# Three steps of lag for the second product, an in-place subtraction in PSUM, two hand-written orders and a store on two queues

## The chip, the cores and the metric

The kernel runs on one NeuronCore of one Trainium2 chip. The metric is the device time of one execution in microseconds (us). Of the core's engines, TensorE (PE) multiplies into PSUM, VectorE (DVE) and ScalarE (ACT) do elementwise work on SBUF and PSUM, GpSimd (POOL) does elementwise work on SBUF, and SyncE (SP) issues the DMA transfers.

## The reference

Local attention with block summaries, then two feed-forward layers, all in fp32 (B 2, H 8, S 768, D 64, so 1536 tokens of width 512):

```python
scores_l = where(|i - j| < 16, q @ k.T / 8, -1e9)
scores_s = q @ max_over_32(k).T / 8 + log(32)
a = softmax(concat(scores_l, scores_s))
x = a @ concat(v, mean_over_32(v))          # 1536 x 512
h = x @ w_in                                # 512 -> 2048
x = (h - tanh(h)) @ w_out                   # 2048 -> 512
out = ((x @ w1) * (x @ w2)) @ w3 @ w_out2   # 512 -> 1024 -> 1024 -> 512
```

## The kernel before

Every large product is made of three float32r products of 512 columns, high x high, high x low and low x high (`split_mm`, lines 224 to 226). So each operand is first split in a high part (a cast, on ACT or POOL) and a low part (a subtraction, on POOL). Weights arrive as 64-bit words; each unit of 128 x 512 is put together by ACT and DVE (`start`, `dve`: two or three DVE operations), then split (`high`, `low`).

**Attention** goes through 24 groups g, three for each pair of heads, in about 27 steps. For one group: PE makes the scores (S), DVE the maxima (M0 to M3), ACT the exponentials (E0 to E3), DVE the reciprocal sum (R), POOL the scaled probabilities (PP, tile pr), PE their transposes (T, tile t), ACT a copy (PB, tile pt), PE the product with the values (V, tile av), ACT the high part of x (XH) and DVE the low part (XL). The tiles t and av have one buffer each, so V of a group waits until XL of the one before has read av. VB on PE and VC on ACT make the block means of v, K0 to K2 those of k, which POOL copies into the tile kt. Between these, PE folds w3 @ w_out2 in 32 parts (W0, W1) of six products (tile w34a); `PLAN["N34"]` tells how many parts a step takes. What each engine does in which order within a step is written out in `PLAN["L"]`, a list of tokens for steps 0 and 1, for 2 to 16 and for the rest.

**The middle** has 48 steps n, four or six slices f of w_in and w_out by three blocks of 512 tokens. `hidden(n)` makes h for one slice on PE, into one of three PSUM banks (tile ph), 12 products; `curve` makes h - tanh(h): ACT takes u = h*h, tanh, a polynomial's term sq and a mask mk, DVE takes h*u (line 714), h - tanh(h) (line 715), the polynomial (line 716) and, one step later, `copy_predicated` (line 698), which puts h - tanh(h) over the polynomial where the mask says so. Its result g is split into gh (ACT) and gl (POOL). `back(n - LAG)` multiplies with w_out, 12 more products (tile x2, x in the trace). LAG is 2 in the kernel before: PE runs hidden(n), then back(n - 2).

**The last stage** (m = 0 to 7) multiplies with w1, w2 and the folded w3 @ w_out2 by seven products in place of eight; `final` adds up the output banks o and stores them, the last one in two halves, a copy by ACT and one by DVE into one tile, both sent by SP. Engines work in program order; nothing reorders the instructions at run time.

Of the kernel before, what the change touches and what calls it, by code (L numbers as in the profile page):

```python
# [43 lines left out]
LAG = 2  # L44
# [7 lines left out]
PLAN = {"cuts": [2, 17], "N34": [0, 0, 0, 0, 0, 1, 2, 1, 1, 0, 2, 1, 2, 2, 2, 0, 0, 3, 3, 1, 1, 2, 1, 3, 1, 2, 3],  # L52
        "MORE": (15, 18, 22, 23), "MOREU": (20, 24, 26),
        "SIGN": (1, 3, 5, 7, 9, 11, 13, 15, 17, 19, 20, 21, 22, 23, 24, 25, 26, 27, 28, 29, 31, 32, 35, 37, 38, 39, 41, 43, 45, 47, 49, 51, 53, 55, 57, 59, 61, 63, 65, 67, 69, 71, 73, 75, 77, 79), "ACT": (0, 4, 8, 16, 22, 25, 27, 29, 33)}
PLAN["L"] = [
# [12 lines left out]
]  # L68
NEG = -8.0 * 1000000000.0
LOG_BLK = 8.0 * 3.4657359027997265  # L70

UMAX = 0.03125
SS, SB, GAM = 0.23012508654699032, 0.2896718893925817, 0.2494235093653836
# [981 lines left out]
```

## Time and profile before

| | us |
|---|---|
| three runs | 578.0, 579.14, 580.85 |
| median | 579.14 |
| profiled execution | 579.49 |
| its span, first to last instruction | 577.8 |
| what lies outside the span | 1.7 |
| PE busy in the span | 559.2 (97%) |

The profile is a record of every instruction of one execution, with the time for which each engine sat idle and what released it. A share of the span tells which engine is used most; where time can be had is told by its idle time, stretch by stretch. The granted clock is TensorE's, as a share of 2.4 GHz: 0.50 is the lower of its two levels, 1.2 GHz.

### The profile page before, as it was taken

How to read it: one execution, taken by the hardware profiler on the slowest of the kernel's cores; microseconds unless marked ns; L12 is line 12 of the kernel's file. 1: busy time of each engine (PE TensorE's matmuls, PEld its weight loads, DVE VectorE, ACT ScalarE, POOL GpSimd, SP SyncE). 2: the span in 40 equal slices, each digit the busy share in tenths (PEclk: the TensorE clock that was granted, in tenths of full speed). 3: DMA queues.
4: the chain of work that ended last, by engine and by line, in shares of the span. 5: the costliest groups of instructions: out<-in, count | busy, mean ns of one | idle time of the engine just before them, and what ended most of it. 6: DMA issues, size and time to landing. Idle time of an engine off the chain costs nothing.

```text
span 577.8 us, 9217 instructions
## 1 busy us (share of the span) xinstructions
PE 559.2 (97%) x3224; PEld 451.2 (78%) x3224; DVE 459.8 (80%) x881; ACT 336.4 (58%) x736; POOL 295.3 (51%) x259
## 2 busy tenths in 40 slices
PE   6898999999999999999999999999999999999997
PEld 5676777777788888888888888888887887888885
DVE  4887789987999999679999969999568587768610
ACT  4888798956978875567867566855233422213110
POOL 4776677753556556216555423457736554616220
PEclk9798999999999999999999999999999999999999
DMA  8987876441333232012323102223000100000021
GB/s 336 354 301 248 299 242 212 127 175 38 109 111 109 77 107 74 0 40 76 105 75 108 36 2 73 74 73 110 1 1 1 73 1 2 0 2 0 1 91 54
DMA packets 18526, 56.56 MB, mean 98 GB/s; under 512 B 1968, under 2 KB 4656, under 8 KB 18480
## 3 DMA queue, kind: packets, MB, share of 16 engines
q1 hardware_dynamic: 18480, 55.98, 29.1%
q8 instruction: 25, 0.41, 0.3%
q14 instruction: 21, 0.17, 0.1%
HBM read 51.64 MB, written 3.15 MB: 95 GB/s over the span
## 4 chain that ended last, share of the span: by engine, by line
PE 84%; DVE 6%; ACT 5%; POOL 2%; issue 2%; POOLq 0%; DVEq 0%; ACTq 0%
PE x L225 7%; PE x L224 7%; PE x L226 7%; PE ph L224 7%; PE ph L226 7%; PE ph L225 7%; PE p_w L224 5%; PE p_w L226 4%; PE p_w L225 4%; PE o L226 4%; PE o L224 4%; PE o L225 4%; PE w L226 2%; PE w L225 2%; PE w L224 2%
## 5 line engine op out<-in xcount | busy, mean ns | idle before, releaser
L229 POOL TENSOR_TENSOR gl<-g,gh 128x512 fp32r<-128x512 f32 x48 | 65.5, 1366 | 131.7 <-ACT gh L693 69.7
L186 POOL TENSOR_TENSOR wl<-dec,wh 128x512 fp32r<-128x512 f32 x72 | 111.5, 1550 | 13.8 <-ACT wh L179 12.4
L225 PE MATMUL x<-gl,wh 128*128 128x512 f32 x192 | 75.1, 391 | 2.2 <-POOL gl L229 2.2
L224 PE MATMUL x<-gh,wh 128*128 128x512 f32 x192 | 75.1, 391 | 1.0 <-ACT gh L693 0.9
L224 PE MATMUL ph<-xh,wh 128*128 128x512 f32 x192 | 74.9, 390 | 0.0
L226 PE MATMUL x<-gh,wl 128*128 128x512 f32 x192 | 74.8, 390 | 0.0
L225 PE MATMUL ph<-xl,wh 128*128 128x512 f32 x192 | 74.8, 389 | 0.0
L226 PE MATMUL ph<-xh,wl 128*128 128x512 f32 x192 | 74.8, 389 | 0.0
L148 DVE SCALAR_TENSOR_TENSOR dec<-raw,dec 128x512 uint32<-128x512 uint32 x48 | 62.8, 1308 | 1.5
L706 ACT ACTIVATE u<-ph 128x512 f32<-128x512 f32 x48 | 28.8, 599 | 47.2 <-PE ph L226 47.2
L714 DVE TENSOR_TENSOR g<-ph,u 128x512 f32<-128x512 f32 x48 | 32.8, 683 | 18.9 <-ACT th L707 18.7
L229 POOL TENSOR_TENSOR s_w<-s_w,s_w 128x512 fp32r<-128x512 f32 x16 | 22.9, 1446 | 43.5 <-ACT s_w L885 23.5
L179 ACT CAST wh<-dec 128x512 fp32r<-128x512 f32 x52 | 32.3, 622 | 21.3 <-DVE dec L148 21.2
L225 PEld LDWEIGHTS x<-gl,wh 128*128 128x128 f32 x192 | 36.1, 188 | 10.6 <-POOL gl L229 3.1
L698 DVE COPY_PREDICATED g<-mk,th 128x512 f32<-128x512 uint32 x48 | 40.9, 852 | 3.8
L224 PEld LDWEIGHTS x<-gh,wh 128*128 128x128 f32 x192 | 36.1, 188 | 9.6 <-ACT gh L693 1.8
L429 ACT ACTIVATE pr<-pr,nm 128x120 f32<-128x120 f32 x96 | 37.7, 396 | 7.5 <-DVE nm L424 7.5
L226 PEld LDWEIGHTS ph<-xh,wl 128*128 128x128 f32 x192 | 36.1, 188 | 7.5
L224 PEld LDWEIGHTS ph<-xh,wh 128*128 128x128 f32 x192 | 36.1, 188 | 7.5
L225 PEld LDWEIGHTS ph<-xl,wh 128*128 128x128 f32 x192 | 36.1, 188 | 7.4
L226 PEld LDWEIGHTS x<-gh,wl 128*128 128x128 f32 x192 | 36.1, 188 | 7.4
L716 DVE SCALAR_TENSOR_TENSOR g<-sq,g 128x512 f32<-128x512 f32 x48 | 39.0, 812 | 0.7 <-ACT sq L712 0.6
(163 smaller groups left out, 1424.9 us busy)
## 6 DMA issues: line engine op xcount, KB each, us to landing
raw<-w SPq DMA_DIRECT2D x32, 512.0 KB
raw<-w_in SPq DMA_DIRECT2D x16, 512.0 KB
raw<-w_out SPq DMA_DIRECT2D x16, 512.0 KB
vg<-vW SPq DMA_DIRECT2D x8, 768.0 KB
raw<-wo SPq DMA_DIRECT2D x8, 512.0 KB
kt<-kT SPq DMA_DIRECT2D x7, 544.0 KB
qt<-qT SPq DMA_DIRECT2D x7, 384.0 KB
out<-u_out SPq DMA_DIRECT2D x6, 256.0 KB
```

The costliest lines, as they stand in the source:

```text
L148: lambda tu=tu, su=su, lo=lo: stt(out=tu, in0=lo, scalar=29, in1=su, op0=ALU.logical_shift_right, op1=ALU.bitwise_or)])
L179: nc.scalar.copy(out=h, in_=self.t[n])
L186: nc.gpsimd.tensor_tensor(out=l, in0=self.t[self.n_low], in1=h[:, :].bitcast(F32), op=ALU.subtract)
L224: mm(out=acc, lhsT=lh, rhs=rh, start=start, stop=False)
L225: mm(out=acc, lhsT=lh, rhs=rl, start=False, stop=False)
L226: mm(out=acc, lhsT=ll, rhs=rh, start=False, stop=stop)
L229: eng.tensor_tensor(out=out, in0=x, in1=high.bitcast(F32), op=ALU.subtract)
L429: nc.scalar.activation(out=pr[g][:, i, :], in_=pr[g][:, i, :], func=AF.Exp, scale=-1.0, bias=nm[g][:, i:i + 1], accum_out=z[g][:, i, :1])
L698: nc.vector.copy_predicated(out=g, mask=mask[:, :].bitcast(U32), data=t)
L706: nc.scalar.activation(out=u, in_=ph, func=AF.Square)
L714: nc.vector.tensor_tensor(out=gn, in0=ph, in1=u, op=ALU.mult)
L716: nc.vector.scalar_tensor_tensor(out=gn, in0=sq, scalar=GAM, in1=gn, op0=ALU.add, op1=ALU.mult)
```

## The change

Five things. LAG becomes 3, with `NG2 = 3` buffers of gh and gl as before. DVE writes h - tanh(h) back into the bank ph, and `copy_predicated` reads it there, so that the bank stays in use until then. The orders `PLAN["L"]`, `N34` and the lists of which weight unit is taken by which engine are other ones; the middle's order is now a table too, `PLAN["MIDDLE"]`, with one row for each of the first eight steps and one for all others. In the last stage, for m of 3 and more, waiting weight units are split ahead of `w34_split`. The last output bank goes through two tiles; ACT issues the store of its half itself.

```diff
-LAG = 2
+LAG = 3
+NG2 = 3
-PLAN = {"cuts": [2, 17], "N34": [0, 0, 0, 0, 0, 1, 2, 1, 1, 0, 2, 1, 2, 2, 2, 0, 0, 3, 3, 1, 1, 2, 1, 3, 1, 2, 3],
+PLAN = {"cuts": [2, 17], "N34": [0, 0, 0, 0, 0, 2, 0, 2, 2, 0, 2, 1, 2, 1, 2, 0, 1, 2, 3, 1, 2, 1, 1, 3, 1, 2, 3],
...
+PLAN["MIDDLE"] = [
+    ["G", "U", "EV", "EV", "HID", "UT", "EV", "H", "EV", "SM", "MM", "RS", "BK", "C"],
...
+    ["HID", "ST", "H", "EV", "C", "U", "UT", "G", "SM", "MM", "L", "RS", "BK"],
...
-                nc.vector.tensor_tensor(out=t, in0=ph, in1=t, op=ALU.subtract)
...
+        def curve_m(n):
+            ph, u, sq, t, mask, gn = curves[n]
+            nc.vector.tensor_tensor(out=gn, in0=ph, in1=u, op=ALU.mult)
+            nc.vector.tensor_tensor(out=ph, in0=ph, in1=t, op=ALU.subtract)
+            nc.vector.scalar_tensor_tensor(out=gn, in0=sq, scalar=GAM, in1=gn, op0=ALU.add, op1=ALU.mult)
+
+        def curve_c(n):
+            ph, u, sq, t, mask, gn = curves[n]
+            nc.vector.copy_predicated(out=gn, mask=mask[:, :].bitcast(U32), data=ph)
...
+        for n in range(NS + LAG):
+            for tok in PLAN["MIDDLE"][min(n, len(PLAN["MIDDLE"]) - 1)]:
+                step(tok, n)
...
+                w = DM // 2
+                for i, tag, copy, q in ((0, "u", nc.scalar.copy, nc.scalar), (w, "gh", nc.vector.tensor_copy, nc.sync)):
+                    o = tmp(tag, f"out_{k}_{j}_{i}", NG2 if tag == "gh" else 2)
+                    copy(out=o[:, :w], in_=acc[k, j][:, i:i + w])
+                    q.dma_start(out=out[rows, i:i + w], in_=o[:, :w])
...
+            if m > 2:
+                wt.high()
+                wt.low()
             w34_split(m)
```

In the table's tokens HID is hidden(n), UT u and tanh, SM sq and mask, MM the three DVE operations, C `copy_predicated` of n - 1, G the split of n - 1, BK back(n - LAG), U, D, ST, H and L the weight units, EV and RS the accumulators.

The program of POOL at the start of attention (pr_1 is PP of group 1, kt_1 the block maxima of the second pair of heads, wl and wh the parts of a weight unit), before:

```order
L441 TENSOR_TENSOR pr_0_198<-pr_0_198,r_0_246 128x480
L365 COPY kt_1_166<-kb_1_278 128x12x24
L186 TENSOR_TENSOR wl_0_283<-dec_0_212,wh_0_282 128x512
L441 TENSOR_TENSOR pr_1_205<-pr_1_205,r_1_293 128x480
L177 CAST wh_1_309<-dec_1_262 128x512
L186 TENSOR_TENSOR wl_1_310<-dec_1_262,wh_1_309 128x512
```

and after:

```order
L455 TENSOR_TENSOR pr_0_189<-pr_0_189,r_0_248 128x480
L379 COPY kt_1_166<-kb_1_261 128x12x24
L455 TENSOR_TENSOR pr_1_207<-pr_1_207,r_1_291 128x480
L200 TENSOR_TENSOR wl_0_295<-dec_0_214,wh_0_294 128x512
L191 CAST wh_1_321<-dec_1_266 128x512
L200 TENSOR_TENSOR wl_1_322<-dec_1_266,wh_1_321 128x512
```

The scaled probabilities of group 1 have moved ahead of the low part of weight unit 0.

The program of PE from V of group 12 (av_12; its second row is VB) to the scores before V of group 13, before (the two rows of scores come once more, then V of group 13):

```order
L463 MATMUL av_12_1230<-pt_12_1141,vg_4_762 64x64 x8
L380 MATMUL av_12_1230<-vg_5_983,mean_89 32x128 x12
L448 MATMUL t_14_1267<-ident_66,pr_14_1110 120x128 x4
L414 MATMUL s_17_27_1291<-kt_5_758,qt_5_974 64x120 x2
L414 MATMUL s_17_28_1292<-kt_5_758,qt_5_974 64x120 x2
```

and after:

```order
L477 MATMUL av_12_1238<-pt_12_1153,vg_4_816 64x64 x8
L394 MATMUL av_12_1238<-vg_5_1045,mean_89 32x128 x12
L238 MATMUL w34a_0_6_1121<-wh_3_414,wh_11_988 128x512
L239 MATMUL w34a_0_6_1121<-wl_3_415,wh_11_988 128x512
L240 MATMUL w34a_0_6_1121<-wh_3_414,wl_11_989 128x512
L238 MATMUL w34a_0_7_1125<-wh_3_414,wh_11_988 128x512
L239 MATMUL w34a_0_7_1125<-wl_3_415,wh_11_988 128x512
L240 MATMUL w34a_0_7_1125<-wh_3_414,wl_11_989 128x512
L462 MATMUL t_14_1281<-ident_66,pr_14_1093 120x128 x4
L428 MATMUL s_17_27_1302<-kt_5_702,qt_5_897 64x120 x2
L428 MATMUL s_17_28_1303<-kt_5_702,qt_5_897 64x120 x2
```

A part of the fold now stands between these two V; before, two parts stood behind V of group 13.

The program of PE at the end of hidden(2), before (gh_1 and gl_1 are the parts of g of step 0):

```order
L225 MATMUL ph_2_2074<-xl_0_127,wh_26_1923 128x512
L226 MATMUL ph_2_2074<-xh_0_124,wl_26_1924 128x512
L224 MATMUL x2_0_0_2113<-gh_1_2056,wh_27_1953 128x512
L225 MATMUL x2_0_0_2113<-gl_1_2057,wh_27_1953 128x512
L226 MATMUL x2_0_0_2113<-gh_1_2056,wl_27_1954 128x512
```

and after:

```order
L239 MATMUL ph_2_2065<-xl_0_127,wh_26_1926 128x512
L240 MATMUL ph_2_2065<-xh_0_124,wl_26_1927 128x512
L238 MATMUL ph_3_2096<-xh_0_124,wh_27_1954 128x512
L239 MATMUL ph_3_2096<-xl_0_127,wh_27_1954 128x512
L240 MATMUL ph_3_2096<-xh_0_124,wl_27_1955 128x512
```

The 12 products of hidden(3) now stand ahead of back(0). DVE at the same place, from weight unit 29 (dec_29) to `copy_predicated` of step 0, before:

```order
L144 TENSOR_SCALAR dec_29_1935<-dec_29_1935 128x512
L146 SCALAR_TENSOR_TENSOR dec_29_1935<-raw_29_1880,dec_29_1935 128x512
L148 SCALAR_TENSOR_TENSOR dec_29_1935<-raw_29_1880,dec_29_1935 128x512
L321 TENSOR_TENSOR w34_6_122<-w34a_1_6_1867,w34_6_122 128x512
L321 TENSOR_TENSOR w34_7_123<-w34a_1_7_1871,w34_7_123 128x512
L229 TENSOR_TENSOR xl_2_129<-av_23_1972,xh_2_126 128x256
L714 TENSOR_TENSOR g_0_2032<-ph_0_2015,u_0_2028 128x512
L715 TENSOR_TENSOR th_0_2030<-ph_0_2015,th_0_2030 128x512
L716 SCALAR_TENSOR_TENSOR g_0_2032<-sq_0_2029,g_0_2032 128x512
L698 COPY_PREDICATED g_0_2032<-mk_0_2031,th_0_2030 128x512
```

and after:

```order
L335 TENSOR_TENSOR w34_6_122<-w34a_1_6_1865,w34_6_122 128x512
L335 TENSOR_TENSOR w34_7_123<-w34a_1_7_1869,w34_7_123 128x512
L243 TENSOR_TENSOR xl_2_129<-av_23_1964,xh_2_126 128x256
L158 TENSOR_SCALAR dec_29_1960<-dec_29_1960 128x512
L160 SCALAR_TENSOR_TENSOR dec_29_1960<-raw_29_1876,dec_29_1960 128x512
L162 SCALAR_TENSOR_TENSOR dec_29_1960<-raw_29_1876,dec_29_1960 128x512
L718 TENSOR_TENSOR g_0_2024<-ph_0_2007,u_0_2020 128x512
L719 TENSOR_TENSOR ph_0_2007<-ph_0_2007,th_0_2022 128x512
L720 SCALAR_TENSOR_TENSOR g_0_2024<-sq_0_2021,g_0_2024 128x512
L724 COPY_PREDICATED g_0_2024<-mk_0_2023,ph_0_2007 128x512
```

The weight unit has moved behind the end of the fold and the last XL, and the subtraction writes ph. On ACT the cast of this unit moves from ahead of u to between tanh and sq of step 0. In steps 7 to 20 the same weight units are put together some three steps later than before, one step ahead of the first product that reads them.

## Rows read from the trace of the kernel before

**Rows 1.** The page: busy time by engine; TensorE's granted clock in 40 slices.

```profile
PE 559.2 (97%) x3224; PEld 451.2 (78%) x3224; DVE 459.8 (80%) x881; ACT 336.4 (58%) x736; POOL 295.3 (51%) x259
PEclk9798999999999999999999999999999999999999
```

**Rows 2.** Stretches: length, busy of PE, PEld, DVE, ACT, POOL; clock, DMA share, GB/s.

```profile
20.00:24.00 4.00, 4.00 (x54) 3.05 (x48) 2.93 (x14) 2.56 (x10) 3.78 (x5) 0.50 1.05 423
...
40.00:44.00 4.00, 3.23 (x56) 2.06 (x54) 3.56 (x17) 4.00 (x18) 3.09 (x4) 1.00 0.99 299
44.00:48.00 4.00, 3.02 (x42) 2.38 (x43) 3.17 (x15) 3.53 (x12) 2.48 (x3) 0.66 0.96 380
48.00:52.00 4.00, 4.00 (x32) 3.05 (x30) 2.32 (x12) 2.90 (x12) 2.83 (x3) 0.91 0.75 210
```

**Rows 3.** Timeline of PE in attention: start, length, what, idle before it.

```profile
18.30 1.11 PE L448 MATMUL t<-ident,pr 128*120 128x128 f32 x4 [1.14 <-POOL pr L441]
...
29.80 0.65 PE L448 MATMUL t<-ident,pr 128*120 128x128 f32 x4 [0.52 <-POOL pr L441]
...
41.44 0.69 PE L463 MATMUL av<-pt,vg 120*64 120x64 f32 x16
...
44.98 0.91 PE L463 MATMUL av<-pt,vg 120*64 120x64 f32 x16 [1.48 <-DVE xl L229]
...
76.55 0.69 PE L463 MATMUL av<-pt,vg 120*64 120x64 f32 x16 [1.22 <-DVE xl L229]
77.17 0.50 PE L224 MATMUL w34a<-wh,wh 128*128 128x512 f32 x1
...
80.02 0.60 PE L448 MATMUL t<-ident,pr 128*120 128x128 f32 x4
```

**Rows 4.** Timeline of POOL at the start.

```profile
16.03 1.27 POOL L186 TENSOR_TENSOR wl<-dec,wh 128x512 fp32r<-128x512 f32 x1
17.26 0.98 POOL L441 TENSOR_TENSOR pr<-pr,r 128x480 f32<-128x480 f32 x1
```

**Rows 5.** Timeline of PE at the start of the middle.

```profile
120.07 0.50 PE L224 MATMUL ph<-xh,wh 128*128 128x512 f32 x1
...
130.82 0.49 PE L225 MATMUL x<-gl,wh 128*128 128x512 f32 x1 [0.85 <-POOL gl L229]
...
149.28 0.50 PE L225 MATMUL x<-gl,wh 128*128 128x512 f32 x1 [1.32 <-POOL gl L229]
...
151.91 0.39 PE L224 MATMUL ph<-xh,wh 128*128 128x512 f32 x1
...
157.35 0.39 PE L224 MATMUL ph<-xh,wh 128*128 128x512 f32 x1
```

**Rows 6.** Timeline of DVE, ACT and POOL there, in step 0.

```profile
121.53 0.41 DVE L144 TENSOR_SCALAR dec<-dec 128x512 uint32<-128x512 uint32 x1
...
122.71 1.67 DVE L148 SCALAR_TENSOR_TENSOR dec<-raw,dec 128x512 uint32<-128x512 uint32 x1
124.30 1.27 DVE L321 TENSOR_TENSOR w<-w34a,w 128x512 f32<-128x512 f32 x2
...
127.25 0.68 DVE L716 SCALAR_TENSOR_TENSOR g<-sq,g 128x512 f32<-128x512 f32 x1
128.04 0.73 DVE L698 COPY_PREDICATED g<-mk,th 128x512 f32<-128x512 uint32 x1
...
128.80 0.62 ACT L693 CAST gh<-g 128x512 fp32r<-128x512 f32 x1 [1.01 <-DVE g L698]
...
129.50 1.27 POOL L229 TENSOR_TENSOR gl<-g,gh 128x512 fp32r<-128x512 f32 x1 [3.09 <-ACT gh L693]
```

**Rows 7.** DVE by line and form, 160 to 225 us: count, busy us, mean ns.

```profile
L148 DVE SCALAR_TENSOR_TENSOR dec<-raw,dec 128x512 uint32<-128x512 uint32 x12 | 17.4, 1450 | 0.4
L698 DVE COPY_PREDICATED g<-mk,th 128x512 f32<-128x512 uint32 x12 | 12.8, 1066 | 1.2
```

**Rows 8.** Timeline of PE in the last stage, and of ACT, SP and DVE at the end.

```profile
444.13 0.50 PE L226 MATMUL w<-xh,wl 128*128 128x512 f32 x1 [0.17 <-POOL wl L186]
...
574.29 0.37 ACT L839 COPY gl_out<-o 128x256 f32<-128x256 f32 x1 [10.52 <-PE o L226]
574.69 0.81 SPq L842 DMA_DIRECT2D out<-gl_out  x2
574.70 0.42 DVE L841 COPY gl_out<-o 128x256 f32<-128x256 f32 x1 [5.25 <-ACT gl_out L839]
```

More of the change, by code (lines that the diff above doesn't have):

```diff
@@ new lines, in fused_kernel, with curve_u, curve_s @@
+        curves = {}
+        def curve_u(n, ph):
+            u, sq, t, mask, gn = (tmp(z, n) for z in ("u", "sq", "th", "mk", "g"))
+            nc.scalar.activation(out=u, in_=ph, func=AF.Square)
+            nc.scalar.activation(out=t, in_=ph, func=AF.Tanh)
+            curves[n] = ph, u, sq, t, mask, gn
+        def curve_s(n):
+            ph, u, sq, t, mask, gn = curves[n]
+            nc.scalar.activation(out=sq, in_=u, func=AF.Square, scale=SS, bias=nsb[:])
+            nc.scalar.activation(out=mask, in_=u, func=AF.Relu, bias=numax[:])
@@ L788, in fused_kernel @@
         NS = len(seq)
-        cur = None
         ab = [(NS + i) % 3 for i in range(3)]
-        for n in range(NS + LAG):
-            nxt = hidden(n) if n < NS else None
-            if n == NS:
-                a = product_a(0, 0)
-            if n == NS + 1:
-                pb = half("w2", 0, 0)
-                w34_split(0)
-            if n < FIRST:
-                cur = curve(n, nxt, cur)
-            wt.start()
-            if n == NS + 1:
-                prev = 0, 0, product_b(0, 0, a, pb)
-            if LAG <= n < FIRST:
-                wt.unit()
-            if n >= LAG:
-                wt.high()
-            closing = len(evac)
-            evacuate()
-            if n >= FIRST:
-                cur = curve(n, nxt, cur)
-            wt.low()
-            if not closing:
-                resplit(2)
-            if n >= LAG:
-                back(n - LAG)
+        phs, passed = {}, set()
@@ new lines, in fused_kernel, with once, step @@
+        tail = {}
+        def once(tok, n, *first):
+            if not 0 <= n < NS or (tok, n) in passed:
+                return False
+            assert all((x, n) in passed for x in first), (tok, n)
+            passed.add((tok, n))
+            return True
+        def step(tok, n):
+            if tok == "HID":
+                if once(tok, n):
+                    phs[n] = hidden(n)
+                if n == NS:
+                    tail["a"] = product_a(0, 0)
+                if n == NS + 1:
+                    tail["b"] = half("w2", 0, 0)
+                    w34_split(0)
+            elif tok == "UT":
+                if once(tok, n, "HID"):
+                    curve_u(n, phs.pop(n))
+            elif tok == "SM":
+                if once(tok, n, "UT"):
+                    curve_s(n)
+            elif tok == "MM":
+                if once(tok, n, "UT", "SM"):
+                    curve_m(n)
+            elif tok == "C":
+                if once(tok, n - 1, "MM"):
+                    curve_c(n - 1)
+            elif tok == "G":
+                if once(tok, n - 1, "C"):
+                    curve_g(n - 1)
+            elif tok == "BK":
+                if once(tok, n - LAG, "G"):
+                    back(n - LAG)
+            elif tok == "ST":
+                wt.start()
+                if n == NS + 1 and "prev" not in tail:
+                    tail["prev"] = 0, 0, product_b(0, 0, tail.pop("a"), tail.pop("b"))
+            elif tok == "D":
+                wt.dve()
+            elif tok == "U":
+                wt.unit()
+            elif tok == "H":
+                wt.high()
+            elif tok == "L":
+                wt.low()
+            elif tok == "EV":
+                tail["closing"] = len(evac)
+                evacuate()
+            elif tok == "RS":
+                if not tail["closing"]:
+                    resplit(2)
+            else:
+                raise KeyError(tok)
@@ L834, in final @@
                     continue
-                o = tmp(("u", "u", "gh", "gl")[j], f"out_{k}_{j}", LAG + (j > 1))
-                w = DM // 2 if k == NTB - 1 and j == TB // P - 1 else DM
-                for i in range(0, DM, w):
-                    if j % 2 and i == 0:
-                        nc.scalar.copy(out=o[:, i:i + w], in_=acc[k, j][:, i:i + w])
-                    else:
-                        nc.vector.tensor_copy(out=o[:, i:i + w], in_=acc[k, j][:, i:i + w])
-                    nc.sync.dma_start(out=out[k * TB + j * P:k * TB + (j + 1) * P, i:i + w], in_=o[:, i:i + w])
+                rows = slice(k * TB + j * P, k * TB + (j + 1) * P)
+                if k < NTB - 1 or j < TB // P - 1:
+                    o = tmp(("u", "u", "gh", "gl")[j], f"out_{k}_{j}", NG2 if j > 1 else 2)
+                    (nc.scalar.copy if j % 2 else nc.vector.tensor_copy)(out=o, in_=acc[k, j])
+                    nc.sync.dma_start(out=out[rows, :], in_=o)
+                    continue
+                w = DM // 2
[3 more added lines that the diff above has]
+                    q.dma_start(out=out[rows, i:i + w], in_=o[:, :w])
         H = KC // 2
```

44 lines of the change are left out of this document (14 added, 30 removed), and 33 rows, old and new, of the table PLAN.

## The prediction

> **What bounds the kernel now.** I read the page's busy shares first: PE is busy for 97% of the span [rows 1], so time can come only from PE's own gaps, from its clock, or from the end after its last product. The granted clock, in 40 slices of 14.4 us, is below 9 tenths only in slices 2 and 4 [rows 1]. So everything that can be had lies before about 160 us, with small change at the end. I then read stretches of 4 us to place the low clock: 0.50 at 20 to 24 us, and 0.66 and 0.91 at 44 to 52 [rows 2]. Last, the timeline of PE with its idle times: in attention PE waits at the transposes of group 1 (1.14 us) and group 4 (0.52), at V of group 6 (1.48, for XL) and of group 13 (1.22, for XL) [rows 3]; at the start of the middle it waits for gl twice, 0.85 and 1.32 [rows 5]. Afterwards 24 products take 5.44 us, from 151.91 to 157.35 [rows 5], 0.227 us each, and PE runs like that nearly to the end.
>
> **Start of attention.** POOL's scaled probabilities of group 1 started at 17.26, behind a low part of a weight that took from 16.03 to 17.26, and released PE at 18.30 [rows 4, 3]. The new program has the probabilities first. The gain is at most PE's wait, 1.14, and nothing if their other operand, R on DVE, comes no earlier than before. I take the middle, 0.6. The low part that is passed is next needed by the first fold product, behind V of group 1; PE's work up to there hides it.
>
> **Attention's order.** No product is added or removed; parts of the fold are moved. Two parts took from 77.17 to 80.02 [rows 3], 1.43 us each. A step in which PE has little work is one in which it waits, since V of a group needs XL of the one before, and ACT and DVE have about as much to do per group as PE: ACT is busy for all of 40 to 44 us [rows 2]. From V of group 5 (41.44) PE had only a transpose and scores before V of group 6, and needed 3.54 us for that [rows 3]. In the new order this place looks the same, but between V of groups 1 and 6 there stand six parts instead of five: one part, 1.43, against a wait of 1.48. Between V of groups 12 and 13 one part now stands where none was: 1.43 against a wait of 1.22. I take both waits as gone, 2.7 us. In return V of group 3 now follows V of group 2 with only a transpose and scores between. Its price lies between nothing (the part ahead of V of group 2 has given ACT and DVE time) and the 1.48 that the same pattern cost at group 6. I take 0.7, half of it. The 0.52 at group 4 I leave. Together -2.0, with bounds of -3.2 (that too gone) and +1.5.
>
> **The clock.** After PE's long wait at 44.98 the clock fell: 0.34 of 4 us and 0.09 of the next 4 [rows 2] are 1.7 us of PE's time. After the wait of 1.22 at 76.55 it didn't fall: all slices from there are 9 [rows 1]. So with shorter waits I take the 1.7 as gained. The low stretch at 20 to 24, after the start's gaps, I leave as it is: those gaps shrink by 0.6 but stay.
>
> **Lag of 3 at the start of the middle.** From 120.07 to 151.91 PE does six hidden and four back, 120 products, in 31.84 us [rows 5]; at 0.227 each they are 27.2. So 4.6 us are lost there, a little more than the idle time named, as the first product after a wait is also slower. With the new order hidden(3) comes before back(0), and each later back has one hidden more ahead of it, 2.72 us. That covers the waits of back(1) to back(3) whole. Two places are left.
> First, hidden(3) goes to the bank of h of step 0, and that is now in use until `copy_predicated` of step 0 has read it. This is the wait that the change adds; behind it on PE stands back(0). PE gets there at 120.07 + 36 x 0.227 = 128.2. Before, `copy_predicated` ran from 128.04 to 128.77, behind the polynomial at 127.25 [rows 6]. Weight unit 29, the fold's end and XL have only changed places on DVE, so their sum stays, but the unit's operation of 1.67 [rows 6] ran beside a low part on POOL and now starts after it; at 0.7, like its neighbours' 0.68, that is 1.0 earlier. ACT's cast of the unit, 0.62 like the one at 128.80 [rows 6], now delays sq. So the end lies between 127.7 and 129.4, and PE's wait between 0 and 1.2.
> Second, back(0) is reached at 131.0. ACT now does step 1's four functions before gh of step 0, some 2.4 us at the 0.6 of its cast, so gh starts at 129 to 131 and gl, which came 0.7 behind gh and took 1.27 [rows 6], ends at 131 to 133. If hidden(3) was late, so is this place, by as much.
> I take 0.5 left in all and 4.1 gained; bounds 3.0 and 4.6.
>
> **The subtraction in PSUM.** The in-place write has no row; nearest is the polynomial, 0.68, with SBUF output [rows 6]. `copy_predicated` took 0.73 alone and 1.07 on average at 160 to 225 us [rows 6, 7], where it runs beside POOL. I take 0.68 and 0.73, and nothing for the end, since PE covers DVE there. If DVE gets slower, PE waits in steps 15 to 20, where units are now put together one step ahead (rival 3).
> The Trainium skill, "SBUF — State Buffer" (SBUF: two separate sides), says that a DVE operation with two SBUF inputs and a GpSimd operation shut each other out for the whole instruction. The spread between 0.73 and 1.07 agrees with it. By that rule `copy_predicated` with its data in PSUM would stay at 0.73, which speaks against rival 3; the sum stays.
>
> **Weight units ahead of the fold's split.** PE waited 0.17 at 444.13 for a weight's low part and had a slow product [rows 8]. The low part now comes first: -0.2, bounds 0 and -0.4. The split that it passes is needed one `final` later.
>
> **The last bank.** ACT's copy ran from 574.29 and DVE's from 574.70 to 575.12, released by ACT's; SP issued the first half at 574.69, and both together took 0.81 [rows 8]. The new program still has DVE wait for ACT, although they now write two tiles: both read one bank. So the second half is ready at the same time, and SP's first issue, about 0.4, had ended by then. Gain 0, bounds -0.4 (the copies run together after all) and +0.3 (a queue that ACT hasn't used before starts slower).
> The Trainium skill speaks against this part: "DMA: Bandwidth & Descriptors" (Issuing engines are not separate DMA queues) says that a second issuing engine saves only issue time, and "PSUM — Partial Sum Buffer" (PSUM bank collisions raise a hardware error) that two engines may not be in the same bank and partitions at once. By these two the end gives 0, and without them 0.4.
>
> **The sum.** -0.6 - 2.0 - 1.7 - 4.1 - 0.2 = -8.6 on the profiled execution's 579.49 gives 570.9. That execution was 0.35 above the median of 579.14, so against the median 570.5.
>
> **Rivals.**
> 1. *Attention gives nothing back.* The parts moved leave gaps elsewhere, since ACT and DVE set the pace; for it speaks ACT's 4.00 of 4 [rows 2]. The middle and the last stage alone, -4.3: 574.8.
> 2. *The middle's wait only moves* to hidden(3) and back(0). Both late as in the upper bounds, and the next back too: gain 1.5 instead of 4.1: 573.1.
> 3. *Weights come late.* DVE's long operations take 1.45 and 1.07 on average at 160 to 225 [rows 7]. If `copy_predicated` rose to the 1.67 seen beside POOL [rows 6], 0.6 more in each of 13 steps is 7.8, less the 2.7 by which a product with w_out stands behind hidden: PE loses 5: 575.6.
> 4. *Three short places in attention wait* (V of groups 3, 6 and 12 at 1.5 each, and the clock falls as at 44.98): 4.5 + 1.7 against the 2.7 + 1.7 of now, +1.8, beside -4.3: 576.6. For it: V of group 6 is reached by the same three instructions as before.
> 5. *Slower: the clock stays down.* After the start's gaps the clock came back only with PE's work from 18.30 on, which had no wait until 29.80 [rows 3]. The new order has short places early, at V of groups 2 and 3. If these waits hold the clock at 0.50 from 24 to 44 us, PE's 20 us there cost 10 more. With everything else as forecast but the 2.0 of the order: 570.5 + 2.0 + 10 = 582.5. Nothing is won from 13 us more of lower clock on (6.6 lost, with the order's 2.0 gone). Against it: the two fold parts that now stand at V of group 1 and before V of group 2.
>
> **How the numbers follow.** Forecast 0.50 (568 to 573.5), rival 1 0.20, rival 2 0.08, rival 3 0.07, rival 4 0.10, rival 5 0.05. Half a per cent, about what a measurement of this kernel tells from no change, is 2.9 us: faster is below 576.2. The forecast, rivals 1 and 2 and most of 3 are: 0.83. Rival 4 and the rest of 3 are within it: 0.11. Slower, rival 5 and mishaps like it: 0.06. The range reaches from 566.5 (all lower bounds) to 577, which takes in rivals 1 to 4.
>
> **What would show it.** PE's first product of the middle at about 116 instead of 120.07, with no wait above 1 us at V of groups 6 and 13 and the clock at 1.00 from 44 to 52; back(3) ended some 4 us sooner after that start than 31.84; `copy_predicated` near 0.73 throughout; DVE's last copy still behind ACT's. The forecast is wrong if hidden(3) waits more than 1.2 us, if wl or wh release PE between 195 and 230 us, or if the clock is down for longer than now before 60 us.

## The result and the profile after

| | before | after |
|---|---|---|
| median of six executions | 578.89 | 572.16 |
| lowest to highest | 578.0 to 580.85 | 571.32 to 573.32 |
| profiled execution, its span | 579.49, 577.8 | 572.8, 571.1 |

The ratio is 0.9881, with a 95% interval of 0.9863 to 0.9899: 6.7 us faster (5.8 to 7.9). The forecast was 570.5 with a range of 566.5 to 577.

The page of the changed kernel, where [rows 1] stood: busy time by engine, and TensorE's clock in 40 slices.

```profile
PE 556.0 (97%) x3224; PEld 450.0 (79%) x3224; DVE 456.1 (80%) x880; ACT 335.1 (59%) x739; POOL 292.0 (51%) x257
PEclk9899999999999999999999999999999999999999
```

Stretches of the changed kernel, with the columns of [rows 2]:

```profile
20.00:24.00 4.00, 2.22 (x44) 1.55 (x44) 3.83 (x16) 4.00 (x17) 2.85 (x4) 1.00 0.99 365
24.00:28.00 4.00, 2.86 (x20) 2.43 (x21) 3.90 (x19) 3.54 (x15) 3.87 (x5) 0.64 1.03 399
...
44.00:48.00 4.00, 4.00 (x80) 3.23 (x80) 3.76 (x16) 3.24 (x11) 0.99 (x1) 1.00 0.66 217
48.00:52.00 4.00, 4.00 (x44) 2.90 (x43) 3.25 (x14) 4.00 (x16) 2.90 (x4) 1.00 0.87 331
```

PE's timeline at the start of attention, at the first product of the middle, and at the start of back(0):

```profile
17.45 0.65 PE L462 MATMUL t<-ident,pr 128*120 128x128 f32 x4 [1.44 <-POOL pr L455]
...
19.31 0.69 PE L477 MATMUL av<-pt,vg 120*64 120x64 f32 x16 [0.64 <-DMA vg<-vr]
...
22.65 0.65 PE L462 MATMUL t<-ident,pr 128*120 128x128 f32 x4 [1.65 <-POOL pr L455]
...
25.14 1.12 PE L477 MATMUL av<-pt,vg 120*64 120x64 f32 x16 [1.27 <-DVE xl L243]
...
117.66 0.50 PE L238 MATMUL ph<-xh,wh 128*128 128x512 f32 x1
...
128.70 0.39 PE L238 MATMUL x<-gh,wh 128*128 128x512 f32 x1
```

Three things are to be seen. The waits of 1.48 and 1.22 of [rows 3] are gone, and the stretch at 44 to 52 runs at the full clock. In their place PE waits 0.64, 1.65 and 1.27 between 19 and 25 us, and the clock is down at 24 to 28. And from 117.66 on PE does 132 products in 30 us, hidden(3) and back(0) without a wait, where before it did 112. Besides the two waits for gl of [rows 5] the kernel before has a third one there, for gh, at the first product of back(0):

```profile
129.47 0.50 PE L224 MATMUL x<-gh,wh 128*128 128x512 f32 x1 [0.95 <-ACT gh L693]
```

The span is thus best cut at the first product of the middle. Before, it starts at 120.07, and from it to the start of the last product are 453.74 us; after, 117.66 and 449.45. So 2.4 us came from attention and 4.3 from the rest. All further runs are read by these two numbers.

### The profile page after: what moved, and what is told of

Its sections match the earlier page's. It is cut to its first block, busy times and chain, and to the rows that moved or that the text cites. A ratio compares the mean times of both kernels' runs of the same rounds, so it can differ in the third digit from the quotient of the medians.

```text
span 571.1 us, 9225 instructions
## 1 busy us (share of the span) xinstructions
PE 556.0 (97%) x3224; PEld 450.0 (79%) x3224; DVE 456.1 (80%) x880; ACT 335.1 (59%) x739; POOL 292.0 (51%) x257
## 4 chain that ended last, share of the span: by engine, by line
PE 81%; DVE 9%; issue 3%; ACT 3%; DMA 2%; SPq 1%; POOL 0%; DVEq 0%; ACTq 0%
PE ph L238 7%; PE ph L239 7%; PE ph L240 7%; PE x L238 7%; PE x L239 7%; PE x L240 7%; PE p_w L238 5%; PE p_w L240 5%; PE p_w L239 4%; PE o L240 4%; PE o L239 4%; PE o L238 4%; PE w34a L238 2%; DMA raw<-wo 2%; PE w34a L239 2%
## 5 line engine op out<-in xcount | busy, mean ns | idle before, releaser
L162 DVE SCALAR_TENSOR_TENSOR dec<-raw,dec 128x512 uint32<-128x512 uint32 x48 | 48.6, 1013 | 1.5
L718 DVE TENSOR_TENSOR g<-ph,u 128x512 f32<-128x512 f32 x48 | 33.0, 687 | 17.6 <-ACT th L708 16.1
L720 DVE SCALAR_TENSOR_TENSOR g<-sq,g 128x512 f32<-128x512 f32 x48 | 45.3, 943 | 0.6 <-ACT sq L713 0.5
L193 ACT CAST wh<-dec 128x512 fp32r<-128x512 f32 x54 | 33.7, 624 | 15.9 <-DVE dec L162 15.7
L724 DVE COPY_PREDICATED g<-mk,ph 128x512 f32<-128x512 uint32 x48 | 36.0, 749 | 3.9
```

The lines of the kernel that those rows point to most:

```text
L162: lambda tu=tu, su=su, lo=lo: stt(out=tu, in0=lo, scalar=29, in1=su, op0=ALU.logical_shift_right, op1=ALU.bitwise_or)])
L193: nc.scalar.copy(out=h, in_=self.t[n])
L718: nc.vector.tensor_tensor(out=gn, in0=ph, in1=u, op=ALU.mult)
L720: nc.vector.scalar_tensor_tensor(out=gn, in0=sq, scalar=GAM, in1=gn, op0=ALU.add, op1=ALU.mult)
L724: nc.vector.copy_predicated(out=gn, mask=mask[:, :].bitcast(U32), data=ph)
```

## Experiments

Each time is a median, each ratio is to executions of the kernel before on the same chip in the same series. The last two columns come from one profile each: the start of the middle's first product, and the time from there to the start of the last product.

| run | time | ratio, 95% interval | first product of the middle | first to last product |
|---|---|---|---|---|
| old attention, new middle | 578.90 | 0.9989 (0.9972 to 1.0007) | 120.46 | 453.79 |
| new attention, old middle | 585.42 | 1.0096 (1.0075 to 1.0117) | 118.35 | 462.59 |
| old attention, new middle, one unit less | 575.72 | 0.9939 (0.9917 to 0.9962) | 118.42 | 450.06 |
| new attention, old middle, one unit more | 577.77 | 0.9976 (0.9958 to 0.9994) | 117.05 | 454.93 |
| new kernel, lag of 2 | 600.08 | 1.0355 (1.033 to 1.0381) | 117.52 | 475.33 |
| old kernel, lag of 3 | 582.01 | 1.0053 (1.0032 to 1.0074) | 118.65 | 457.34 |
| the same, units from step 2 on | 584.64 | 1.0083 (1.0059 to 1.0107) | 117.84 | 458.18 |
| new kernel, subtraction in SBUF | 573.19 | 0.9886 (0.9867 to 0.9905) | 117.68 | 450.16 |
| new kernel, old tail | 572.92 | 0.9905 (0.9878 to 0.9932) | 119.29 | 449.86 |
| new kernel, raw_2 early | 572.04 | 0.9888 (0.9866 to 0.9911) | 118.18 | 449.45 |
| and steps 2 to 4 in another order | 576.09 | 0.9955 (0.9938 to 0.9972) | 121.83 | 449.48 |
| and raw_3 early, other order | 571.78 | 0.9872 (0.984 to 0.9904) | 116.23 | 449.48 |

### Attention and the middle apart

The first run takes the changed kernel with the old plan of attention, the second the kernel before with the new one.

The lines of `PLAN["L"]`, `"N34"`, `"SIGN"` and `"ACT"` change as in the diff of the change, and with them two lists that will matter; in the first run:

```diff
-        "MORE": (15, 18, 22), "MOREU": (20, 24, 32),
+        "MORE": (15, 18, 22, 23), "MOREU": (20, 24, 26),
```

> The changed kernel with the attention plan of the kernel before (L, N34, MORE, MOREU, SIGN, ACT), so that only the middle's lag and order, the subtraction in PSUM, the split ahead of the fold's and the end are new. My theory, that attention and the middle add up: the middle alone is worth the 4.6 us of waits and slow products that the trace of after no longer has, and attention's 2.4 (start, waits, clock) is missing, so the time stands 4.3 to 4.9 below the kernel before, near 574.4; PE's waits of 1.48 and 1.22 at V of groups 6 and 13 are back, and there is no wait above 0.3 between the first product of the middle and back(3). The rival, that the middle's gain rests in part on attention's new end, where weight unit 29 goes behind the fold's end on DVE: the old plan makes h - tanh(h) of step 0 late by the unit's operation of 1.67 us beside POOL, hidden(3) or back(0) waits 1 to 2 us, and the time is 575.5 to 576.5.

> The kernel before with the attention plan of the changed kernel alone: lag of 2, the old order of the middle, the subtraction in SBUF, the old end. By my theory of added parts it gains attention's 2.4 us and nothing else: near 576.5 (575.8 to 577.3), PE's first product of the middle at 117 to 118.5, and the two waits for gl at the start of the middle remain at 0.8 to 1.4 us each. By the rival, that attention and the middle depend on each other, the middle's waits change here by over 1 us in sum and the time is under 575.5 or over 577.5.

Neither half is worth anything alone: 0.9989, which can't be told from no change, and 1.0096, which is slower. My theory of added parts failed. In the first run PE's timeline has one wait at the start of the middle:

```profile
131.50 0.79 PE L236 MATMUL ph<-xh,wh 128*128 128x512 f32 x1 [2.54 <-DVE g L722]
```

That is hidden(3) waiting for its bank, the wait that the change adds. DVE's timeline of the same run shows what came ahead of `copy_predicated` (L722):

```profile
126.30 0.86 DVE L156 TENSOR_SCALAR dec<-dec 128x512 uint32<-128x512 uint32 x1
127.19 0.69 DVE L158 SCALAR_TENSOR_TENSOR dec<-raw,dec 128x512 uint32<-128x512 uint32 x1
127.92 0.69 DVE L160 SCALAR_TENSOR_TENSOR dec<-raw,dec 128x512 uint32<-128x512 uint32 x1
...
130.72 0.73 DVE L722 COPY_PREDICATED g<-mk,ph 128x512 f32<-128x512 uint32 x1
```

These three operations are a weight unit, number 30. The old plan has done unit 29 in attention already, so the token U in the middle's first row takes the next. Behind the wait the clock was down as well:

```profile
124.00:132.00 8.00, 5.46 (x23) 4.25 (x23) 7.67 (x12) 4.96 (x10) 1.60 (x2) 0.94 0.49 185
132.00:140.00 8.00, 8.00 (x31) 6.44 (x30) 7.11 (x12) 7.42 (x14) 5.51 (x4) 0.84 0.01 3
```

0.06 and 0.16 of 8 us are 1.8; with the 2.54 that is 4.3, all that the middle gained in the changed kernel. The second run has the opposite fault, one unit too few. Its waits of PE (engine, tile and line, what was waited for: us in total, times, longest):

```profile
PE x L228 <- POOL wl L188: 4.9, 2, 4.3
PE x L226 <- ACT wh L181: 2.9, 1, 2.9
```

### The count of weight units at the seam

If that is the cause, one unit moved should mend each half. To the run with the old attention:

```diff
-    ["G", "U", "EV", "EV", "HID", "UT", "EV", "H", "EV", "SM", "MM", "RS", "BK", "C"],
+    ["G", "EV", "EV", "HID", "UT", "EV", "H", "EV", "SM", "MM", "RS", "BK", "C"],
```

To the run with the new attention:

```diff
-        "MORE": (15, 18, 22), "MOREU": (20, 24, 32),
+        "MORE": (15, 18, 22, 23), "MOREU": (20, 24, 26),
```

> Old attention with the new middle (as the first of these runs), but without the token U in the first row of the middle's table, so that one weight unit (unit 30, which the old attention plan leaves to that place as it has already done unit 29) is put together three steps later, where the changed kernel does it. My theory: the 2.54 us for which hidden(3) waited there came from these three operations of DVE (0.86 + 0.69 + 0.69, and ACT's cast) ahead of step 0's; without them the predicated copy of step 0 ends 2.2 us sooner, hidden(3) waits at most 0.6, the low clock behind the wait is gone too, the middle and the last stage take 449.5 to 450.5 us from the first product to the last (453.8 before), and the time stands 4 to 5 us below the kernel before, 573 to 575. Then lag and attention do add up, once the count of units at the seam is right. The rival, that the old end of attention itself is late (unit 29 ahead of the fold's end and the last XL): hidden(3) waits over 1 us still, and the time is over 576.

> New attention with the old middle (as the second of these runs), but with the old lists MORE and MOREU, so that unit 29 is put together at the end of attention, as in the kernel before. My theory: the waits of 2.91, 0.62 and 4.31 for parts of weights came from that one unit, which the new plan leaves to the middle; with it the middle runs as in the kernel before, with its waits for gh and gl of 0.8 to 1.4, some 453.7 us from the first product to the last, and attention's own gain of 1 to 2 us shows: 576.5 to 578. The rival, that the new attention leaves DVE or the transfers behind in more than this unit: waits for weights over 1 us remain, and the time is 580 or more.

Both came out nearly as expected in their traces. In the first, hidden(3) waits a tenth as long:

```profile
127.16 0.50 PE L236 MATMUL ph<-xh,wh 128*128 128x512 f32 x1 [0.28 <-DVE g L722]
```

From the first to the last product it takes 450.06 us instead of 453.79. Its time of 575.72 is a little above the 573 to 575 that I gave; the profiled execution had 574.16. In the second, it takes 454.93 from the first to the last product, 1.2 more than I gave; the waits for weights are gone and those of the old middle are back, the one for gh longer than the 1.4 that I gave as the most:

```profile
PE x L226 <- ACT gh L695: 1.8, 1, 1.8
...
PE x L227 <- POOL gl L231: 1.2, 2, 0.8
```

So with the seam mended the new middle alone is worth 3.5 us (2.2 to 4.8) and the new attention alone 1.4 (0.3 to 2.4). Their sum of 4.9 is less than the 6.7 measured together; the intervals allow for that, and the runs don't settle whether something of it is real.

### The lag without the order, the order without the lag

First the changed kernel with a lag of 2, then the kernel before with a lag of 3 (and three buffers of gh and gl, as it had):

```diff
-LAG = 3
+LAG = 2
```

```diff
-LAG = 2
+LAG = 3
```

and then the latter with two of its rules held at step 2:

```diff
-            if LAG <= n < FIRST:
+            if 2 <= n < FIRST:
...
-            if n >= LAG:
+            if n >= 2:
```

> The changed kernel with LAG = 2 and nothing else: the same table for the middle, back(n - 2) where back(n - 3) stood. My theory, that the third step of lag is what took the waits away: PE reaches back(0) 2.72 us sooner, near 126 in the trace, and gl of step 0 is done near 128.8, so about 2.9 us are lost there, and up to 2 more at back(4), where gl came 12.7 us behind the end of hidden(4) and 10.9 are covered; the time is 575 to 578.5. The rival, that the new order within the steps did it and the lag is only room: waits under 1 us in the first six steps and a time under 573.4.

> The kernel before with LAG = 3 alone (three buffers of gh and gl, as before): old attention, old order within the steps, subtraction in SBUF, old end. My theory after the last four runs: the lag gives room for gl and, more than that, for the weights with w_out, whose parts are due one step later; the bank of h of step 0 is free here as soon as DVE's subtraction into SBUF has read it, before PE reaches hidden(3). So all three waits at the start of the middle (0.95, 0.85, 1.32) go, 4 to 4.6 us with the slow products behind them, none comes in their place, and the time is 574 to 575.5. The rival, that lag and order only work together: a wait for gl or for a weight's parts of over 1 us stays in the first ten steps, and the time is 576.5 or more.

> The kernel before with LAG = 3, as in the run of the lag alone, but with the two rules of the middle that start the weight units at step LAG held at step 2. In the run of the lag alone DVE put no weight together between 127 and 140, though it waited 1.7 us in each step there, and the unit of back(2) was begun at 140.25, when PE stood before it (waits of 2.12, 0.70 and 2.07). My theory: those waits came from this rule alone, which the new table undoes as well; with the units from step 2 on they go, and the three waits for gh and gl are gone through the lag: the middle and the last stage take 449.5 to 450.5 us from the first product to the last (453.7 in the kernel before, 457.3 with the lag alone), and the time is 574 to 576. The rival, that the lag needs the new order within the steps as well: waits over 1 us for gl or for weights remain, 452 us or more, and 577 or more.

I was wrong in all three, and always on the same side. With a lag of 2 the waits for gh and gl came, somewhat smaller than I gave (1.3 and 0.9, where I had 2.9 for both), but they are the small part. The waits of PE there:

```profile
PE x L240 <- POOL wl L200: 13.9, 5, 4.3
...
PE ph L240 <- POOL wl L200: 1.6, 1, 1.6
```

The new table puts units together one step ahead, and with the second product one step earlier they are late, by 4.3 us in each of three steps between 215 and 244 us.

With the lag of 3 in the old order all waits for gl and gh go, and weights come late instead. PE's timeline:

```profile
142.83 0.50 PE L224 MATMUL x<-gh,wh 128*128 128x512 f32 x1 [2.12 <-ACT wh L179]
144.25 0.50 PE L226 MATMUL x<-gh,wl 128*128 128x512 f32 x1 [0.70 <-POOL wl L186]
...
152.06 0.50 PE L226 MATMUL x<-gh,wl 128*128 128x512 f32 x1 [2.07 <-POOL wl L186]
```

I put that down to the rule that starts the units at step LAG, and the third run takes it away. The waits for weights did go. But a wait for gl of the old size is there again, and behind it PE came to the accumulators of the next block sooner than ACT had emptied them; PE's rows, and ACT's timeline of the same run:

```profile
147.07 0.50 PE L225 MATMUL x<-gl,wh 128*128 128x512 f32 x1 [1.32 <-POOL gl L229]
...
157.83 0.50 PE L224 MATMUL x<-gh,wh 128*128 128x512 f32 x1 [4.59 <-ACT x2a L740]
```

```profile
153.96 0.62 ACT L693 CAST gh<-g 128x512 fp32r<-128x512 f32 x1 [1.02 <-DVE g L698]
...
156.67 0.62 ACT L179 CAST wh<-dec 128x512 fp32r<-128x512 f32 x1 [0.29 <-DVE dec L148]
157.20 2.04 ACT L740 COPY x2a<-x 128x512 f32<-128x512 f32 x4
```

The four copies stand behind the load and the cast of a weight unit, which waits for DVE, some 1.4 of the 4.59; for the rest ACT was late itself, with gh, sq and mk of the step before still to do from 153.96 on, where gh had waited for `copy_predicated`. In the new table's row for this step the token U stands behind EV, and in the changed kernel the copies ran at 148.64, with no wait of PE:

```profile
148.64 2.04 ACT L753 COPY x2a<-x 128x512 f32<-128x512 f32 x4
```

So the rival held: the lag needs the order, in three places at least, the units, the accumulators and the curve.

### The subtraction in SBUF, and the old tail

```diff
-            nc.vector.tensor_tensor(out=ph, in0=ph, in1=t, op=ALU.subtract)
+            nc.vector.tensor_tensor(out=t, in0=ph, in1=t, op=ALU.subtract)
...
-            nc.vector.copy_predicated(out=gn, mask=mask[:, :].bitcast(U32), data=ph)
+            nc.vector.copy_predicated(out=gn, mask=mask[:, :].bitcast(U32), data=t)
```

> The changed kernel with h - tanh(h) written to SBUF, in the tile of tanh, as before, and read from there by the predicated copy; all else as in the changed kernel. My theory, that the write to PSUM shortens DVE's operation but doesn't touch the end, since PE covers DVE there: the predicated copy's mean goes back from 749 ns to some 850 and its longest from 769 to over 1600, and the time is that of the changed kernel within 1.2 us (571 to 573.4). The rival, that DVE was near its limit in the middle: PE waits there again for gl or for a weight's parts, 2 to 6 us in all, 574 to 578.

The time is the same within the intervals. `copy_predicated` by itself, first in the changed kernel, then with the data in SBUF (shortest, median and longest in ns, and when):

```profile
L724 DVE COPY_PREDICATED g<-mk,ph x48: 723/752/769, 124.9 to 375.4; 128x512 f32<-128x512 uint32 x48
```

```profile
L724 DVE COPY_PREDICATED g<-mk,th x48: 739/763/1710, 125.0 to 376.0; 128x512 f32<-128x512 uint32 x48
```

The operation itself isn't faster (752 against 763); what goes is the long cases. The mean rises to 969, more than the 850 that I gave, DVE's total from 456.1 to 465.5, and PE has no new wait in the middle. The Trainium skill, "SBUF — State Buffer" (SBUF: two separate sides), says that a DVE operation with two SBUF inputs and a GpSimd operation that reads SBUF hold a shared port in turn, each for its whole length; longest cases of 1710 with two SBUF inputs and of 769 with one agree. But the waiting partly moved: the polynomial (L720), which still has two SBUF inputs, has a mean of 943 in the changed kernel and of 818 here, while the weight units' last operation (L162) goes the other way, 1013 and 1217.

The next run puts both halves of the last bank in one tile again, stored by SP, as in the kernel before, and takes out the early split:

```diff
-            if m > 2:
-                wt.high()
-                wt.low()
             w34_split(m)
```

> The changed kernel without the split of waiting weight units ahead of the fold's, and with the old end (one tile for both halves of the last bank, both stores from SP). My theory, that both edits are worth nothing: the short wait near 407 us goes and the one that stood at 444.13 in the kernel before comes back some 7 us sooner, near 437, with 0.2; from the last product's start to the end of the span it stays 3.99 us; the time is that of the changed kernel within 1 us (571.2 to 573.2). The rival, that one of the two edits pays: 0.4 to 1 us more at the end, or waits of over 0.5 in the last stage, and a time over 573.2.

As expected for the end: from the start of the last product to the end of the span it is 4.0 us, as in both kernels. The split ahead of the fold's did not move the short wait near 407, and only took away the one near 439; this run has both:

```profile
408.85 0.50 PE L239 MATMUL o<-w34l,gh_c 128*128 128x512 f32 x1 [0.18 <-POOL w34l L243]
...
439.47 0.50 PE L240 MATMUL w<-xh,wl 128*128 128x512 f32 x1 [0.17 <-POOL wl L200]
```

From first to last product it is 449.86 against 449.45, 0.4 us, which the times don't resolve.

### The start of attention

Where do the new waits at 19 to 25 us come from? In the changed kernel ACT stands for a weight unit's load, and DVE's R and POOL's PP of group 2 follow late (one row each of ACT, DVE and POOL):

```profile
19.08 0.64 ACT L145 ACTIVATE bits<-raw 128x512 f32<-128x512 f32 x1 [1.93 <-DMA raw<-wo]
```

```profile
21.10 0.15 DVE L450 TENSOR_REDUCE r<-z 128x4 f32<-128x8 f32 x1
```

```profile
21.61 0.99 POOL L455 TENSOR_TENSOR pr<-pr,r 128x480 f32<-128x480 f32 x1 [1.07 <-DVE r L451]
```

The first run moves that load up:

```diff
             load_q(1)
-            wt.load(2)
+            wt.load(3)
```

The second also moves tokens in steps 2 to 4 (R and PP first, XL right behind XH) and loads kt_2 behind the block means; here the new head of these steps and the end of step 1:

```diff
+    [("R", 1), ("PP", 1), ("L", 0), ("K0", -2), ("XH", 4), ("XL", 4), ("M3", 0),
...
+     ... ("BR", 0), ("LK", -5), ("PB", 3)],
```

The third keeps kt_2 there, but loads raw_3 sooner, leaves step 4 as it was, puts R and PP behind the maxima in step 3, and PB ahead of H in step 2:

```diff
-                    wt.ahead = min(NRAW, g + 2)
+                    wt.ahead = min(NRAW, g + 3)
```

> The changed kernel with one transfer moved: the load of weight unit 2 (raw_2) is issued before those of vg_1 and kt_2 instead of behind them. My theory of attention's new waits: ACT stands 1.93 us for raw_2, and with it DVE's R of group 2 (queued behind that unit's two operations) and POOL's PP, which released PE 1.65 late at the transposes of group 2. With raw_2 some 1.3 MB sooner in the queue, near 4 us at the 340 GB/s of that stretch, ACT doesn't wait, PP of group 2 starts near 20.5 instead of 21.61, PE's wait at T of group 2 falls to 0.3 to 0.7, and the time is 1 to 2 us under the changed kernel, 570 to 571. The rival, that the transfers as a whole are late: vg_1 or the block means (vg from vr) then release V of group 0 later by as much, and the time stays at 572.

> The run with raw_2 early, and besides: kt_2 is loaded behind the block means of v, and in steps 2 to 4 R and PP stand first and XL right behind XH, ahead of the next group's maxima. By my theory this takes most of what PE still waits at the start: T of group 1 near 16.0 instead of 17.45, V of group 0 near 17.7 to 18.5 instead of 19.31 since kt_2 no longer stands ahead of it in the queue, and V of group 1 without its 1.27; if PE has no wait over 0.6 behind 20 us, the clock stays at 1.00 there and its 1.7 us come back too. The time is 568 to 570. The rival, that the order moves the wait: ACT's and DVE's work per group is the same, so V of groups 2 to 4 waits instead, or kt_2 comes too late for K of the third pair of heads; 571 to 574.

> The changed kernel with another start of attention: raw_2 and raw_3 are loaded right before and behind vg_1, kt_2 behind the block means of v; in step 2 R and PP stand first and PB ahead of the weight's cast, in step 3 R and PP stand behind the maxima and ahead of the weight unit. The last version of this kind lost 4 us where ACT stood 3.75 for raw_3, which kt_2 had overtaken; here it can't. My theory that the in-order wait for raw loads on ACT is what makes PE wait at the start: T of group 1 near 16.3 (17.45 in the changed kernel), T of group 2 near 20.4 (22.65), V of group 1 near 22.5 to 23.5 (25.14), the middle begins near 116 instead of 117.5 to 119.3, and the time is 569.5 to 571. The rival, that the start is bound by the transfers as a whole (340 to 370 GB/s throughout): what comes sooner makes something else later (vg_1, kt_2 or raw_3), PE's waits up to 30 us sum to as much as before, and the time is 571.5 to 573.5.

With raw_2 early PP of group 2 started at 20.47 and the wait at T of group 2 went, as I said, but the time stayed, so by the time the rival held. PE still waits at V of groups 0 and 1, at V of group 1 longer than before:

```profile
20.21 1.12 PE L477 MATMUL av<-pt,vg 120*64 120x64 f32 x16 [0.57 <-DMA vg<-vr]
26.44 0.69 PE L477 MATMUL av<-pt,vg 120*64 120x64 f32 x16 [1.53 <-DVE xl L243]
```

ACT's timeline of this run tells why V of group 1 waits. ACT now stands for the next load, raw_3, and XH of group 0, which XL follows, has its place behind it:

```profile
23.71 0.64 ACT L145 ACTIVATE bits<-raw 128x512 f32<-128x512 f32 x1 [3.34 <-DMA raw<-wo]
```

The second run, where kt_2 is issued ahead of raw_3, made this larger; a row of ACT, and what became of it at PE's scores:

```profile
24.51 0.62 ACT L145 ACTIVATE bits<-raw 128x512 f32<-128x512 f32 x1 [3.75 <-DMA raw<-wo]
```

```profile
27.83 1.06 PE L428 MATMUL s<-kt,qt 64*64 64x120 f32 x12 [3.63 <-DVE nm L438]
```

The middle began at 121.83, some 4 us late, and the time rose by 4. But ACT stood nearly as long in the first run, 3.34, and there the middle began at 118.18. What differs besides is the order: R, which needs ACT's exponentials, now stands ahead of the next group's maxima, so DVE stood 4.74 us for it and the scores waited for DVE. So the load alone doesn't account for the 4 us, and no run takes load and order apart. The Trainium skill, "DMA: Bandwidth & Descriptors" (Queues, rings and completion order), says that each DMA engine takes the descriptors of one queue in their order; that ACT's wait for raw_3 ended 0.8 us later with kt_2 ahead of it (24.51 against 23.71) agrees, but doesn't prove it, since the block means ahead of both were issued 0.57 later as well.

In the third run ACT has no wait for either load: T of group 1 stands at 16.52, T of group 2 has no wait, PE's idle time up to 30 us is 8.50 where the changed kernel has 10.24, and the middle begins at 116.23, the earliest of all. Its time, 571.78, is the lowest, but it misses the 569.5 to 571 that I gave, lies in the rival's range and can't be told from the changed kernel's. So ACT's wait for loads does reach PE, by a way that the order decides and not one for one; what it is worth in time isn't shown. V of group 0 still waits for the block means of v, which are issued behind all earlier loads:

```profile
19.79 0.69 PE L477 MATMUL av<-pt,vg 120*64 120x64 f32 x16 [1.12 <-DMA vg<-vr]
```

## Why the prediction was right, and where it was not

**What bounds the kernel: right.** All of the gain lies before 150 us, and PE's share stayed at 97%.

**Start of attention, -0.6: right at T of group 1, and gone by V of group 1.** T came 0.85 sooner, at 17.45 instead of 18.30, as the probabilities did, at 16.41 instead of 17.26. My condition, nothing if R comes no earlier, was wrong: R's last operation came 0.2 later. These are DVE's row before, and DVE's and POOL's after:

```profile
15.86 0.18 DVE L437 RECIPROCAL r<-r 128x4 f32<-128x4 f32 x1
```

```profile
16.08 0.18 DVE L451 RECIPROCAL r<-r 128x4 f32<-128x4 f32 x1
```

```profile
16.41 0.99 POOL L455 TENSOR_TENSOR pr<-pr,r 128x480 f32<-128x480 f32 x1 [1.49 <-ACT wh L193]
```

But V of group 1 starts at 25.14, no sooner than before:

```profile
25.11 0.69 PE L463 MATMUL av<-pt,vg 120*64 120x64 f32 x16
```

**Attention's order, -2.0: right behind V of group 1, and a price ahead of it that I put at nothing.** Both waits that I took as gone went (2.7 us), and V of group 3, for which I charged 0.7, had none. What I missed stands earlier: 0.64, 1.65 and 1.27 at V of group 0, T of group 2 and V of group 1. PE's idle time from T of group 1 to the middle rose by 0.6 instead of falling by 2.0. This is not an accident of one execution, as the means of five profiles of the old attention plan and six of the new one show:

| | old | new |
|---|---|---|
| start of T of group 1 | 18.5 | 17.6 |
| from there to V of group 1 | 6.3 | 8.0 |
| PE's idle time in it, lowest to highest | 0.0 to 0.4 | 2.6 to 3.6 |
| from V of group 1 to the middle | 94.3 | 92.3 |
| PE's idle time in it, lowest to highest | 4.0 to 4.7 | 1.0 to 1.5 |

So behind V of group 1 the order is worth the 2.0, and up to there it loses 1.7, more than the start had won. PE's idle time overstates the loss: from 20 to 24 us PE ran at a clock of 0.50 before [rows 2], busy throughout, and after at 1.00, with its waits. The step that failed is that I followed PE, ACT and DVE through the new order, but not SP and ACT's own wait for a load: ACT stood 1.93 us for raw_2, with one of group 2's exponentials and R behind it. That this wait is all of the reason is not shown: in the old plan ACT stood for the same load too (0.82 before, up to 1.75 in another profile), and PE had no such waits.

**The clock, -1.7: the size fits the two profiles, the reason doesn't hold, and that is luck.** The fall at 44 to 52 that I tied to the wait of 1.48 does not follow from that wait alone. In the kernel before with a lag of 3 the wait is there, at 44.94, and the same stretches run at full clock:

```profile
44.00:48.00 4.00, 3.06 (x49) 2.62 (x50) 3.15 (x15) 3.56 (x12) 2.44 (x3) 1.00 1.03 402
48.00:52.00 4.00, 4.00 (x46) 2.86 (x45) 3.51 (x17) 3.27 (x13) 3.19 (x4) 1.00 0.80 243
```

Of five profiles of the old attention one has the fall, so the 1.7 was that profile's own. The middle began at 117.84 to 120.46 in these five (mean 119.1) and at 117.05 to 119.29 in six of the new one (mean 117.9). So attention is worth some 1.2 us, with a standard error of 0.6, not the 2.4 of the two profiles that I compared, and the profile from which I predicted was on the late side of its kind.

**Lag of 3 at the middle's start, -4.1: right in size (4.3), too simple in its reason.** The waits for gl went as told, and hidden(3) didn't wait, at the good end of my 0 to 1.2. I had overlooked the wait of 0.95 for gh: the 4.6 is not a little more than the idle time of 2.17 that I named, but 1.5 more than the 3.12 of all three. But I charged the lag alone with the gain. The runs show that this wait is 2.54 with one weight unit more ahead of it, that units or accumulators come late when the lag is 3 in the old order, and that the new order with a lag of 2 loses 28 us. I had written rival 3, weights that come late, as a matter of DVE's long operations in steps 15 to 20, with 0.07; they decide at the seam, by the count of units there, and with a lag of 2 also at 212 to 244 us, near the steps that I named.

**PSUM, the split in the tail, the last bank, 0, -0.2 and 0: right.** `copy_predicated` took 0.75 throughout, the end 4.0 before and after, and DVE's copy still starts only behind ACT's, as these rows of the end of the changed kernel show:

```profile
567.11 0.40 PE L240 MATMUL o<-w34h,c 128*128 128x512 f32 x1
...
567.54 0.37 ACT L893 COPY u_out<-o 128x256 f32<-128x256 f32 x1 [10.46 <-PE o L240]
567.94 0.37 ACTq L894 DMA_DIRECT2D out<-u_out  x1
568.01 0.42 DVE L893 COPY gh_out<-o 128x256 f32<-128x256 f32 x1 [5.26 <-ACT u_out L893]
568.46 0.33 SPq L894 DMA_DIRECT2D out<-gh_out  x1
```

The last issue waits for DVE's copy as it did in [rows 8]; an issue saved on SP isn't late enough to matter. Nor did ACT's queue, new to it, cost the 0.3 of my upper bound: the issue took 0.37, SP's 0.33. The 0.17 of the split was won, as the run without it shows, but a wait of 0.18 at 407 us is new; all profiles with a lag of 3 have one like it, at 406 to 416, and none with a lag of 2 has.

**The sum.** -8.6 forecast, -6.7 measured. Between the two profiles it is -0.85 up to T of group 1, +0.9 from there to V of group 1, -2.4 from there to the middle, where I had -3.7 for order and clock, and -4.3 behind it. That the sum came so near is in part luck: the clock's 1.7 belongs to the profile from which I predicted.

## What to carry to other kernels

A longer lag between two products moves every due time behind it: of weights, of accumulators, of buffers. Before it is charged with a gain, count at the seam what each in-order engine has to have done, since one weight unit too many or too few there cost 3.7 or 7.7 us. A gain at one place should be followed to the next place where PE waits: 0.85 won at T of group 1 was gone by V of group 1. A gap of PE seen in one profile should be looked for in a second one before a clock that falls behind it is put into a sum.

## What was unexpected of the hardware

The clock. The same attention plan, with the same wait of 1.48 at V of group 6, runs through the first 52 us in several ways: the low level lay within 16 to 28 and 44 to 52 in the profile before, only before 28 us in four others of this plan; in the new plan at 24 to 32 in the changed kernel (0.64 and 0.93), and longer in the run with the old tail (0.76, 0.81, 0.62 and 0.53 from 16 to 32), where the middle began 1.6 us later although PE sat idle no longer. Over whole executions it shows as well: the run with old attention and new middle took 576.2 us at a mean clock of 0.997 and 581.6 at 0.987, on the same chip. What decides which way it goes no run here shows.
